# Last stage of a transformer block: order of two first loads, PSUM tags of one plain product, and two banks for the last accumulator

## The chip, the core and the metric

The kernel runs on one core of one Trainium2 chip. The metric is device time in microseconds (us) of one execution; the median of eight runs of the kernel before is 760.04 us (758.58 to 761.81). Engines are named as in the profile: PE is TensorE, DVE is VectorE, ACT is ScalarE, POOL is GpSimd, SP is SyncE. SP and ACT also issue DMA transfers, each from its own queue, in the order of their programs.

## The reference

Input x is 2048 tokens by 1024 features in bf16. The block is

```
h  = x + linear_attention(layernorm(x)) @ wo
h2 = h + (relu(g) * u) @ W_down       where g = layernorm(h) @ W_gate, u = layernorm(h) @ W_up
```

W_gate and W_up are 1024 by 3584, W_down is 3584 by 1024. The change touches the last product alone, called the Down stage here: with hh = relu(g) * u (2048 by 3584), it computes out = h + hh @ W_down.

## The kernel before

Each large product is done by the Winograd form of Strassen's scheme: both matrices are cut into 2 by 2 blocks, sums and differences of blocks are formed, and seven block products take the place of eight. In the Down stage this is done on two levels.

**Outer level.** hh is cut into halves of 1024 tokens and 1792 inner features, W_down into halves of 1792 rows and 512 columns. The seven outer products run in the order `OUTER = (1, 2, 6, 5, 3, 7, 4)` (line 808); n is the place in this order, from 0 to 6. The block sums of the left side were written to DRAM by the stage before ("spilled", `x_dram`, lines 661 and 668) and come back by `load_x` (line 833); W_down itself, or sums of its blocks from `t_dram`, come by `load_w` (line 820). One `load_x` or `load_w` is 896 KB: 128 partitions of seven rows of 512 bf16 numbers. A spilled tile is ready in DRAM when its last row has been written; the last row of all is written by line 668 at the very end of the stage before.

**Inner level.** Outer products 2, 6, 5, 3 and 4 (`INNER`) are again done by the seven-product scheme (`inner`, line 1081): each inner product `mm` (line 1098) is 512 tokens by 896 by 256, that is 4 token tiles of 128 times 7 slices of the inner features, 28 matmuls of 128x256. Outer products 1 (n = 0) and 7 (n = 5) are done plainly, in four pieces p of two token tiles, each 2 times 14 matmuls of 128x512 (`plain_mm`, line 930).

**Accumulators.** PSUM holds four accumulators of two banks each ([128, 1024] fp32): two of tag A, one of tag X, one of tag Y. In an inner product m1, m6, m7 and m4 are added up in one A, with a copy taken by DVE between them (`snap`, line 1109, which also adds the running sum `base`); m2 has X or Y by the parity of n (`tag`, line 1084), and so has m5, in the same accumulator as soon as m2 has been read; m3 is added onto m5. A product that adds onto an accumulator must wait for the copy that reads it; a product that takes an accumulator anew must wait for the last reader of its former content. In the plain product at n = 5 the four pieces use A, A, Y and X (line 1244).

**Order.** PE, DVE and ACT run in the order in which the program is written (`manual_schedule`, line 745), SP too in the Down stage (line 964). The sums of an outer product's operands (t1, s1, s2, t2, s4, s3, t3, t4, lines 1018 to 1045) stand in `queue`, and `pop()` puts the next one into DVE's order between the copies. So at n = 1 three such sums of the next product, t1, s1 and s2, stand in DVE's order after the addition "00" that follows m2 and ahead of the copy "s2" (`snap` of u2), which frees A for m7.

**The last outer product** (n = 6, `tail`) has no successor to overlap with. It ends with m7, a copy, m4 in the other A accumulator ("m4f"), additions for the four output quadrants (`sink`, which calls `put`, line 1064), and m3 in two halves of two token tiles ("m3a", "m3b"), each followed by its addition ("01a", "01b"). `put` adds accumulator and copy into a bf16 tile (line 1069), adds h where that was not done earlier (line 1071), and stores with a DMA from ACT's queue (line 1073). m5, m3a and m3b all live in one accumulator of tag X.

Of the kernel before, what the change touches and what calls it, by code (L numbers as in the profile page):

```python
# [31 lines left out]
def block_kernel(ctx: ExitStack, tc: tile.TileContext, x, wqkv, wo, wg, wu, wd, out, H: int):  # L32
# [178 lines left out]
    with ExitStack() as actx:  # L211
# [11 lines left out]
        def load_x(t):  # L223
            x_sb = bwork.tile([P, D], BF16, tag=("x_res", "oT")[atiles.index(t) % 2], bufs=XB, name="x_sb")
            nc.sync.dma_start(out=x_sb[:], in_=xf[t * P:(t + 1) * P, :])
            x_tiles[t] = x_sb

        def load_w(dst, j, col):
            nc.sync.dma_start(out=dst[:, :, j * NW:(j + 1) * NW], in_=wqkv_v[:, :, col + j * NW:col + (j + 1) * NW])
# [744 lines left out]
    def new_op(n):  # L974
        return {"n": n, "k": OUTER[n], "s": {}, "t": {}}
# [18 lines left out]
    def pop(n=1):  # L994
        for _ in range(n):
            if queue:
                queue.pop(0)[2]()
# [63 lines left out]
            nc.scalar.dma_start(out=v[:], in_=h_dram[i][s][:, :, j * DW:(j + 1) * DW])  # L1061
            hres[k, s] = v

    def put(k, s, ts, cs, ps, m, with_h=True):

        i, j = outs[k]
        o = dpool.tile([P, NT * HW], BF16, tag="o", bufs=4, name="o")
        ov = o[:, 0:(ts.stop - ts.start) * (cs.stop - cs.start)].rearrange("p (t d) -> p t d", t=ts.stop - ts.start)
        add(out=ov, in0=ps, in1=m, op=ALU.add)  # L1069
        if with_h:  # L1070
            add(out=ov, in0=ov, in1=hres[k, s][:, ts, cs], op=ALU.add)  # L1071
        t0 = (i * HS + s * SW) // P
        nc.scalar.dma_start(out=out_v[:, t0 + ts.start:t0 + ts.stop, j * DW + cs.start:j * DW + cs.stop], in_=ov)

    def cols(j):
        return slice(j * HW, (j + 1) * HW)
# [4 lines left out]
    def inner(op):  # L1081

        k, st, base = op["k"], {}, base_of[op["k"]]
        tag = "XY"[op["n"] % 2]

        def left(m):
            return {1: x_tile(op["n"], 0, 0), 2: x_tile(op["n"], 0, 1), 3: op["s"].get("s4"), 4: x_tile(op["n"], 1, 1),
                    5: op["s"].get("s1"), 6: op["s"].get("s2"), 7: op["s"].get("s3")}[m]

        def right(m):  # L1090
            w = [w_tile(op["n"], x) for x in range(2)]
            return {1: w[0][:, :, cols(0)], 2: w[1][:, :, cols(0)], 3: w[1][:, :, cols(1)], 4: op["t"].get("t4"),
                    5: op["t"].get("t1"), 6: op["t"].get("t2"), 7: op["t"].get("t3")}[m]

        def view(nm):
            return st[nm][:].rearrange("p (t d) -> p t d", t=NT)

        def mm(m, nm, t=None, ts=range(NT)):
            need(op, *{3: ("s4",), 4: ("t4",), 5: ("s1", "t1"), 6: ("s2", "t2"), 7: ("s3", "t3")}.get(m, ()))
            if t:  # L1100
                st[nm] = acc(t)
            pv = view(nm)
            for tt in ts:
                for f in range(FQ):
                    nc.tensor.matmul(pv[:, tt, :], lhsT=left(m)[:, f, tt * P:(tt + 1) * P], rhs=right(m)[:, f, :],  # L1105
                                     start=(t is not None and f == 0 and tt % 2 == 0),
                                     stop=(f == FQ - 1), skip_group_check=True)

        def snap(nm, s, j):
            st[nm] = dpool.tile([P, NT, HW], FP32, tag="snap", bufs=4, name="snap")  # L1110
            add(out=st[nm][:], in0=view("A"), in1=base[s][:, :, cols(j)], op=ALU.add)  # L1111

        def add_h(m, s, j):
            add(out=st[m][:], in0=st[m][:], in1=hres[k, s][:, :, cols(j)], op=ALU.add)

        def sink(s, j, nm, m, ts=ALL, with_h=True):
            m = base[s][:, ts, cols(j)] if m is None else st[m][:, ts]
            if k in u_of:
                add(out=u_of[k][s][:, ts, cols(j)], in0=view(nm)[:, ts], in1=m, op=ALU.add)
            else:  # L1120
                put(k, s, ts, cols(j), view(nm)[:, ts], m, with_h)

        return {
            "m1": lambda: mm(1, "A", "A"), "s1": lambda: snap("m1", 0, 0), "m2": lambda: mm(2, "D", tag),
            "00": lambda: sink(0, 0, "D", "m1"), "m6": lambda: mm(6, "A"), "s2": lambda: snap("u2", 0, 1),
            "m5": lambda: mm(5, "E", tag), "m7": lambda: mm(7, "A"), "s3": lambda: snap("u3", 1, 1),
            "11": lambda: sink(1, 1, "E", "u3"), "m4": lambda: mm(4, "A"), "10": lambda: sink(1, 0, "A", None),
            "m3": lambda: mm(3, "E"), "01": lambda: sink(0, 1, "E", "u2"),
            "m4f": lambda: mm(4, "F", "A"), "10f": lambda: sink(1, 0, "F", "u3f"), "snap": snap,
            "01a": lambda: sink(0, 1, "E", "u2", slice(0, 2), False),  # L1130
            "01b": lambda: sink(0, 1, "E", "u2", slice(2, 4), False), "h01": lambda: add_h("u2", 0, 1),
            "m3a": lambda: mm(3, "E", None, (0, 1)), "m3b": lambda: mm(3, "E", None, (2, 3)),
        }

    ops = [new_op(n) for n in range(len(OUTER))]
    load_x(1, 1, 1, slice(0, FQ - 1))
    load_x(1, 1, 1, slice(FQ - 1, FQ))
    load_w(1, 0)
    load_w(1, 1)
    load_x(1, 0, 1)  # L1140
    queue_sums(ops[1])

# [24 lines left out]
    for n in range(1, len(OUTER)):  # L1167
        op = ops[n]
        nxt = ops[n + 1] if n + 1 < len(OUTER) else None
        tail = nxt is None  # L1170

        def early_loads():
            if nxt and n > 1:
                load_w(n + 1, 0)
                load_x(n + 1, 1, 0)

        def late_x():
            if nxt and n > 1:
                load_x(n + 1, 1, 1)

        def late_w():
            if nxt and n > 1:
                load_w(n + 1, 1)
                if nxt["k"] in INNER:
                    queue_sums(nxt)

        def ahead():
            if n + 2 < len(OUTER):
                need(op, "s4")
                load_x(n + 2, 0, 0)  # L1190
                load_x(n + 2, 0, 1)

        early_loads()
        if op["k"] in INNER:
            cur = inner(op)
            cur["m1"]()
            if prv:
                prv["11"]()
                pop()
            cur["s1"]()  # L1200
            cur["m2"]()
            if prv:
                prv["m4"]()
            late_x()
            cur["00"]()
            pop()
            if prv:
                prv["10"]()
                prv["m3"]()
            late_w()  # L1210
            pop()
            cur["m6"]()
            if prv:
                prv["01"]()
            pop()
            if nxt:
                load_h(nxt["k"], 0)
                if op["k"] not in outs:
                    load_h(nxt["k"], 1)
            cur["m5"]()  # L1220
            cur["s2"]()
            if tail:
                cur["h01"]()
            pop(2)
            cur["m7"]()
            ahead()
            pop(2)
            if tail:
                cur["snap"]("u3", 1, 1)
                cur["m4f"]()  # L1230
                cur["11"]()
                cur["snap"]("u3f", 1, 0)
                cur["m3a"]()
                cur["10f"]()
                cur["01a"]()
                cur["m3b"]()
                cur["01b"]()
            else:
                cur["s3"]()
            prv = cur  # L1240
        else:
            pss = []
            for p in range(4):
                ps = acc(("A", "A", "XY"[n % 2], "XY"[(n + 1) % 2])[p])
                plain_mm(ps, n, p, 0)
                plain_mm(ps, n, p, 1)
                if p == 0 and prv:
                    prv["11"]()
                    prv["m4"]()
                    late_x()  # L1250
                    prv["10"]()
                    prv["m3"]()
                    late_w()
                    prv["01"]()
                    load_h(op["k"], 1)
                s, t0 = divmod(2 * p, NT)
                ts = slice(t0, t0 + 2)
                v = ps[:].rearrange("p (t d) -> p t d", t=2)
                put(op["k"], s, ts, full, v, u5[s][:, ts, :])
                add(out=u2[s][:, ts, :], in0=v, in1=u2[s][:, ts, :], op=ALU.add)  # L1260
                pop(2)
            if nxt:
                load_h(nxt["k"], 0)
                load_h(nxt["k"], 1)
            prv = None
# [46 lines left out]
```

## Time and profile before

| What | us |
|---|---|
| median of 8 runs | 760.04 (758.58 to 761.81) |
| the profiled execution's own time | 761.81 |
| its span, first to last instruction | 760.0 |
| time around the span | 1.8 |
| PE busy in the span | 731.6 (96%) |
| DVE busy in the span | 567.4 (75%) |
| Down stage in the span | from about 585 to 760 |

Times inside the profile are counted from the start of the span. A line of the timeline has the start, the duration, the engine, the line of the kernel, the operation, the tiles written and read, the shape, the number of merged instructions, and in brackets the idle time of the engine before it with what ended it. Matmuls overlap, so a run of them ends for the next engine a little before its printed end. The granted clock (PEclk) is the share of TensorE's full clock that the chip allowed; it averages 0.987 over the span.

### The profile page before, as it was taken

The numbers are of one execution on the slowest core, as the hardware profiler recorded it, in microseconds if no ns is written. First come the engines' busy times: TensorE is split into PE (matmuls) and PEld (weight loads), VectorE is DVE, ScalarE is ACT, GpSimd is POOL, SyncE is SP. The second block draws the span as 40 slices with busy tenths as digits, with TensorE's granted clock in tenths as the row PEclk, the third lists the DMA queues.
The fourth block names the chain that finished last, engine by engine and source line by source line (L and its number), as shares of the span: only waits on it lengthen the run. The fifth ranks groups of instructions, "written<-read, shape, count | busy, mean of one in ns | idle before, by whom it ended". The sixth has DMA issues, their size and how long they took to land. (4 is left out here: it accounts for less than half of the span.)

```text
span 760.0 us, 10598 instructions
## 1 busy us (share of the span) xinstructions
PE 731.6 (96%) x3967; PEld 385.0 (51%) x4020; DVE 567.4 (75%) x1023; ACT 324.4 (43%) x596; POOL 5.8 (1%) x44
## 2 busy tenths in 40 slices
PE   8999999999889989999999999999999999999986
PEld 3444555444344434444444444444444468887565
DVE  6997645786886756778777787797786398994784
ACT  4785664877777544434344443444443110000000
POOL 0000000000000000000000000000000000000000
PEclk9999999999999999999999999999999999999998
DMA  9755003099767526165628277594482697978631
GB/s 318 168 124 153 1 0 111 1 212 209 175 148 185 126 62 201 42 197 136 199 92 248 99 219 237 179 290 167 161 268 84 235 361 266 328 279 317 209 94 46
DMA packets 146563, 132.03 MB, mean 174 GB/s; under 512 B 50896, under 2 KB 128080, under 8 KB 146512
## 3 DMA queue, kind: packets, MB, share of 16 engines
q1 hardware_dynamic: 134848, 122.97, 53.2%
q10 hardware_dynamic: 11664, 8.39, 3.6%
q8 instruction: 31, 0.51, 0.3%
q14 instruction: 20, 0.16, 0.1%
HBM read 79.95 MB, written 39.85 MB: 158 GB/s over the span
## 5 line engine op out<-in xcount | busy, mean ns | idle before, releaser
L783 ACT ACTIVATE gu<-gu 128x512 bf16<-128x512 bf16 x72 | 45.4, 630 | 131.9 <-DVE gu L782 127.4
L778 ACT COPY snap<-accA 128x1024 f32<-128x1024 f32 x72 | 72.4, 1008 | 37.0 <-PE accA L773 37.0
L536 PE MATMUL attn<-wo_mem,oT 128*128 128x512 bf16 x247 | 59.0, 387 | 4.1 <-DVE o_sb L516 3.2
L773 PEld LDWEIGHTS <-tg 128*128 128x128 f16 x384 | 37.5, 98 | 45.3
L773 PEld LDWEIGHTS <-tu 128*128 128x128 f16 x384 | 37.6, 98 | 45.3
L153 ACT COPY u<-Aq 128x512 f32<-128x512 f32 x56 | 32.2, 581 | 44.6 <-PE Aq L297 19.3
L782 DVE TENSOR_TENSOR gu<-accY,snap 128x1024 bf16<-128x1024 f32 x36 | 43.8, 1218 | 9.8 <-ACT snap L778 9.6
L773 PE MATMUL accA<-hn,tu 128*128 128x512 f16 (+1 forms) x192 | 49.3, 379 | 0.0
L773 PE MATMUL accA<-hn,tg 128*128 128x512 f16 (+1 forms) x192 | 49.3, 379 | 0.0
L782 DVE TENSOR_TENSOR gu<-accX,snap 128x1024 bf16<-128x1024 f32 x36 | 43.9, 1218 | 7.2 <-PE accX L773 4.7
L1105 PEld LDWEIGHTS <-x 128*128 128x128 f16 (+1 forms) x448 | 44.5, 100 | 9.1 <-issue 2.9
L773 PEld LDWEIGHTS <-wg 128*128 128x128 bf16 x288 | 28.2, 98 | 34.9 <-issue 1.1
L773 PEld LDWEIGHTS <-wu 128*128 128x128 bf16 x288 | 28.2, 98 | 34.0
L536 PEld LDWEIGHTS <-oT 128*128 128x128 bf16 x256 | 25.4, 99 | 36.2 <-issue 8.8
L1105 PEld LDWEIGHTS <-xs 128*128 128x128 f16 x308 | 30.2, 98 | 3.6
L786 DVE TENSOR_TENSOR hq<-gu 128x512 bf16<-128x512 bf16 x48 | 20.3, 422 | 14.3 <-ACT gu L783 14.2
L297 PEld LDWEIGHTS <-xT 128*128 128x128 bf16 (+1 forms) x192 | 18.6, 98 | 23.5 <-issue 2.1
L516 DVE TENSOR_TENSOR o_sb<-nd,rd 128x384 bf16<-128x384 f32 (+1 forms) x48 | 22.8, 506 | 8.6 <-ACT rd L515 7.5
L538 DVE SCALAR_TENSOR_TENSOR x_res<-attn,x_res 128x512 bf16<-128x512 f32 x32 | 22.0, 688 | 8.8 <-PE attn L536 8.7
L1111 DVE TENSOR_TENSOR snap<-accA,u 128x1024 f32<-128x1024 f32 x16 | 19.5, 1218 | 11.5 <-PE accA L1105 11.5
L1105 PEld LDWEIGHTS <-xd 128*128 128x128 f16 (+1 forms) x224 | 23.1, 103 | 8.8 <-issue 5.0
L934 PEld LDWEIGHTS <-x 128*128 128x128 bf16 (+1 forms) x168 | 16.4, 98 | 19.8
(225 smaller groups left out, 1417.3 us busy)
## 6 DMA issues: line engine op xcount, KB each, us to landing
x<-x_dram SPq DMA_DIRECT2D x17, 896.0 KB, 8.7
x_dram<-hq SPq DMA_DIRECT2D x28, 512.0 KB, 3.0
wg<-in_B_W_gate_dram SPq DMA_DIRECT2D x14, 512.0 KB, 5.1
wu<-in_B_W_up_dram SPq DMA_DIRECT2D x14, 512.0 KB, 7.2
wraw<-in_B_W_down_dram SPq DMA_DIRECT2D x14, 512.0 KB, 5.1
x_dram<-hq SPq DMA_DIRECT2D x28, 256.0 KB, 2.5
t_dram<-wt SPq DMA_DIRECT2D x28, 256.0 KB, 2.2
xd<-x_dram SPq DMA_DIRECT2D x6, 896.0 KB, 5.9
```

The lines of the kernel that those rows point to most:

```text
L153: nc.scalar.copy(out=snaps[nm, v], in_=A[v][:])
L297: nc.tensor.matmul(ps[:], lhsT=left[m - 1][:, kc, r + v * P:r + (v + 1) * P], rhs=right[m - 1][:, kc, :], start=(start and kc == 0), stop= ...
L516: nc.vector.tensor_tensor(out=ov[:, c0:c0 + n], in0=ndv[:, :, 0:P].rearrange("p k (h e) -> p k h e", h=HPC), in1=rd[:, 0:n, :].unsqueeze(3 ...
L536: nc.tensor.matmul(ps[:], lhsT=st["oT"][:, c, :], rhs=wo_sb[:, c, j * NW:(j + 1) * NW], start=(c == 0), stop=(c == KC - 1))
L538: nc.vector.scalar_tensor_tensor(out=h_sb[:, j * NW:(j + 1) * NW], in0=ps[:], scalar=1.0, in1=h_sb[:, j * NW:(j + 1) * NW], op0=ALU.mult, ...
L773: nc.tensor.matmul(ps[:, v, :], lhsT=w[v][n - 1][:, kc, :], rhs=left[n - 1][:, kc, :], start=(t is not None and kc == 0), stop=(kc == KH - ...
L778: nc.scalar.copy(out=st[nm][:], in_=halves(st["A"]))
L782: add(out=g[:], in0=halves(st[nm]), in1=st[base][:], op=ALU.add)
L783: nc.scalar.activation(out=g[:, 0, :], in_=g[:, 0, :], func=ACT.Relu)
L786: add(out=out[q], in0=st[q][:, 0, :], in1=st[q][:, 1, :], op=ALU.mult)
L1105: nc.tensor.matmul(pv[:, tt, :], lhsT=left(m)[:, f, tt * P:(tt + 1) * P], rhs=right(m)[:, f, :], start=(t is not None and f == 0 and tt % ...
L1111: add(out=st[nm][:], in0=view("A"), in1=base[s][:, :, cols(j)], op=ALU.add)
```

## The change

Four places of the Down stage are edited.

1. Before the loop, the first loads at n = 1 are put in another order: first the weights w(1,0), then the first six rows of the spilled tile x(1,1,1), then the weights w(1,1), and then the last row of x(1,1,1).
2. In the plain product at n = 5 the third piece takes tag X and the fourth Y, in place of Y and X.
3. In the last product, m5 and m3 are written into two accumulators, two token tiles in the first bank of X and two in the first bank of Y (`tail_mm`); the additions that follow (`tail_sink`) go by these halves, and the store of the first half is issued from SP's queue in place of ACT's. m3 is not interrupted by other work any more: it runs as one piece after the addition "11".
4. In the last product, h for the second token half is added ahead of time to the running sum `u2[1]`, in one addition of 128x2048 after "h01"; the separate additions of h after "11" and "10" go.

```
-    def put(k, s, ts, cs, ps, m, with_h=True):
+    def put(k, s, ts, cs, ps, m, with_h=True, eng=nc.scalar):
...
-        nc.scalar.dma_start(out=out_v[...], in_=ov)
+        eng.dma_start(out=out_v[...], in_=ov)
...
+        def tail_mm(m, start):
+            need(op, *{3: ("s4",), 5: ("s1", "t1")}[m])
+            for h in range(2):
+                if start:
+                    st["E", h] = acc("XY"[(op["n"] + h) % 2])
+                for tt in range(2):
+                    for f in range(FQ):
+                        t = 2 * h + tt
+                        nc.tensor.matmul(st["E", h][:, tt * HW:(tt + 1) * HW],
+                                         lhsT=left(m)[:, f, t * P:(t + 1) * P], rhs=right(m)[:, f, :],
+                                         start=(start and f == 0 and tt == 0), stop=(f == FQ - 1),
+                                         skip_group_check=True)
+
+        def tail_sink(s, j, h, m):
+            ts = slice(2 * h, 2 * h + 2)
+            put(k, s, ts, cols(j), st["E", h][:, 0:2 * HW].rearrange("p (t d) -> p t d", t=2), st[m][:, ts],
+                False, (nc.sync, nc.scalar)[h])
...
+            "m5f": lambda: tail_mm(5, True), "m3f": lambda: tail_mm(3, False),
+            "11f": lambda: [tail_sink(1, 1, h, "u3") for h in range(2)],
+            "01f": lambda: [tail_sink(0, 1, h, "u2") for h in range(2)],
...
-            "m4f": lambda: mm(4, "F", "A"), "10f": lambda: sink(1, 0, "F", "u3f"), "snap": snap,
+            "m4f": lambda: mm(4, "F", "A"), "10f": lambda: sink(1, 0, "F", "u3f", ALL, False), "snap": snap,
...
+    load_w(1, 0)
     load_x(1, 1, 1, slice(0, FQ - 1))
+    load_w(1, 1)
     load_x(1, 1, 1, slice(FQ - 1, FQ))
-    load_w(1, 0)
-    load_w(1, 1)
     load_x(1, 0, 1)
...
-            cur["m5"]()
+            cur["m5f" if tail else "m5"]()
             cur["s2"]()
             if tail:
                 cur["h01"]()
+                add(out=u2[1][:], in0=u2[1][:], in1=hres[op["k"], 1][:], op=ALU.add)
...
                 cur["snap"]("u3", 1, 1)
                 cur["m4f"]()
-                cur["11"]()
+                cur["11f"]()
+                cur["m3f"]()
                 cur["snap"]("u3f", 1, 0)
-                cur["m3a"]()
                 cur["10f"]()
-                cur["01a"]()
-                cur["m3b"]()
-                cur["01b"]()
+                cur["01f"]()
...
-                ps = acc(("A", "A", "XY"[n % 2], "XY"[(n + 1) % 2])[p])
+                ps = acc(("A", "A", "XY"[(n + 1) % 2], "XY"[n % 2])[p])
```

More of the change, by code (lines that the diff above doesn't have):

```diff
@@ L1072, in put @@
         t0 = (i * HS + s * SW) // P
-        nc.scalar.dma_start(out=out_v[:, t0 + ts.start:t0 + ts.stop, j * DW + cs.start:j * DW + cs.stop], in_=ov)
+        eng.dma_start(out=out_v[:, t0 + ts.start:t0 + ts.stop, j * DW + cs.start:j * DW + cs.stop], in_=ov)
     def cols(j):
@@ L1128, in inner @@
             "m3": lambda: mm(3, "E"), "01": lambda: sink(0, 1, "E", "u2"),
-            "m4f": lambda: mm(4, "F", "A"), "10f": lambda: sink(1, 0, "F", "u3f"), "snap": snap,
-            "01a": lambda: sink(0, 1, "E", "u2", slice(0, 2), False),
-            "01b": lambda: sink(0, 1, "E", "u2", slice(2, 4), False), "h01": lambda: add_h("u2", 0, 1),
-            "m3a": lambda: mm(3, "E", None, (0, 1)), "m3b": lambda: mm(3, "E", None, (2, 3)),
+            "m4f": lambda: mm(4, "F", "A"), "10f": lambda: sink(1, 0, "F", "u3f", ALL, False), "snap": snap,
+            "h01": lambda: add_h("u2", 0, 1),
         }
     ops = [new_op(n) for n in range(len(OUTER))]
+    load_w(1, 0)
     load_x(1, 1, 1, slice(0, FQ - 1))
+    load_w(1, 1)
     load_x(1, 1, 1, slice(FQ - 1, FQ))
-    load_w(1, 0)
-    load_w(1, 1)
     load_x(1, 0, 1)
```

## The prediction

> **What bounds the kernel now.** The page says PE: 96% busy, and at least nine tenths in nearly every slice of the Down stage. So only PE's waits there, and the work behind its last matmul, can be won. I read PE's waits from 610 to 760 us next. There are three, and the change has one part for each:
>
> ```profile
> PE accX L1105 <- issue: 2.6, 1, 2.6
> PE accX L1105 <- DVE o L1069: 2.5, 1, 2.5
> PE accA L1105 <- DVE snap L1111: 2.1, 1, 2.1
> ```
>
> PE's timeline shows what each wait costs beyond itself:
>
> ```profile
> 627.45 4.88 PE L1105 MATMUL accA<-w,xd 128*128 128x256 f16 x28 [2.11 <-DVE snap L1111]
> 632.17 3.22 PE L1105 MATMUL accA<-wd,x 128*128 128x256 f16 x28
> ...
> 732.48 4.88 PE L1105 MATMUL accX<-wd,x 128*128 128x256 f16 x28 [2.61 <-issue]
> ...
> 753.60 2.55 PE L1105 MATMUL accX<-wd,xd 128*128 128x256 f16 x14 [2.49 <-DVE o L1069]
> ```
>
> 28 matmuls normally print 3.22 us and the next product starts 3.06 us later. After each wait they print 4.88 (1.66 more), and the 14 after the third 2.55 in place of 1.69 (0.86 more). The reason is in the windows; the columns are the stretch and its length, busy time by engine, and then the granted clock:
>
> ```profile
> 218.37:221.78 3.41, 1.69 (x13) 0.97 (x12) 3.41 (x12) 1.44 (x7) 0.00 (x0) 1.00 0.62 92
> 221.78:225.20 3.42, 3.15 (x14) 1.46 (x15) 2.19 (x7) 2.97 (x7) 0.00 (x0) 1.00 0.71 217
> ...
> 624.56:627.97 3.41, 1.30 (x13) 1.01 (x11) 3.41 (x3) 0.00 (x0) 0.00 (x0) 1.00 0.43 102
> 627.97:631.38 3.41, 3.41 (x18) 2.45 (x17) 3.41 (x3) 0.00 (x0) 0.00 (x0) 0.50 0.90 353
> ```
>
> Time is cut into fixed stretches of 3.41 us. A stretch with PE idle for 2.11 us is followed by one at half clock; one with 1.72 us is not, one with 1.90 (201.30 to 204.72) is. I take 1.8. The edges stand fixed in time, so it is chance whether a wait of 2.1 to 2.6 us lies mostly in one stretch. The full price of a half-clock stretch is 1.7 us.
>
> Here the Trainium skill differs ("TensorE: Matmul & The Clock Gate", section "HAM oscillation — how this bites in real kernels"). It says that idle gaps up to about 3.4 us are harmless. By it the 1.66 and 0.86 would not exist, and the sum would hold the third wait and the small costs below alone, 761.81 - 2.49 + 0.5 = 759.8, an estimate; the rows above decide against it.
>
> **Part 1, the loads.** DVE's timeline at n = 1:
>
> ```profile
> 605.64 1.09 DVE L1022 TENSOR_TENSOR ws<-w 128x1792 f16<-128x1792 bf16 x1 [10.03 <-DMA w<-in_B_W_down_dram]
> 606.65 2.02 DVE L1035 TENSOR_TENSOR xd<-xd,x 128x3584 f16<-128x3584 bf16 x1
> ...
> 617.52 1.22 DVE L1111 TENSOR_TENSOR snap<-accA,u 128x1024 f32<-128x1024 f32 x1
> 619.26 1.22 DVE L1069 TENSOR_TENSOR o<-accY,snap 128x1024 bf16<-128x1024 f32 x1 [0.52 <-PE accY L1105]
> ...
> 626.18 1.22 DVE L1111 TENSOR_TENSOR snap<-accA,u 128x1024 f32<-128x1024 f32 x1
> ```
>
> t1 waits for w(1,0), issued at 598.32 and 7.3 us on its way. With w first, issued in the first load's place at 596.11, t1 goes some 5 us earlier. But the backlog does not reach the first wait: DVE idles 0.52 at 619.26 for PE's m2, and from there to the copy's end (619.26 to 627.40, 8.14 us: "00", h, then t1, s1, s2 of the next product, then the copy) it runs without a break, while PE has only m6 and m5, 6.1 us. Nothing in these 8.14 us moves, and DVE's order is the same in the changed kernel. So the first wait stays at 2.11, and part 1 gains nothing.
>
> It may cost. s1 (606.65) needs all of x(1,1,1), whose last row now queues behind both weights. SP held that row until 597.94 (the spill's landing), so it, w(1,1) and x(1,0,1) change places but not in number. In the profile the four loads (2.75 MB) were all in at 598.80 plus 9.4 = 608.2 (the pair of w has a median of 8.4, the first 7.3). If the last row lands as late as that, s1 starts at 608.2 in place of 606.65; if the queue gains from starting on w at once, 606.3. s1 has 0.5 us to spare (the idle time at 619.26). The bounds are 0 and 1.1 us of longer first wait; I take 0.2, since the transfer rate in 597 to 599 was 250 to 270 GB/s against 315 to 345 later, which an earlier w would partly fill. The loads behind keep their place and are released by PE at 601 and 613.
>
> **Part 2, the swap.** Before the last product:
>
> ```profile
> 724.30 1.22 DVE L1260 TENSOR_TENSOR u<-accY,u 128x1024 f32<-128x1024 f32 x1
> ...
> 731.16 1.22 DVE L1260 TENSOR_TENSOR u<-accX,u 128x1024 f32<-128x1024 f32 x1
> 732.29 1.08 DVE L1029 TENSOR_TENSOR wd<-wd 128x1792 f16<-128x1792 f16 x1
> 733.29 1.08 DVE L1032 TENSOR_TENSOR ws<-wd,ws 128x1792 f16<-128x1792 f16 x1
> 734.30 1.22 DVE L1111 TENSOR_TENSOR snap<-accA,u 128x1024 f32<-128x1024 f32 x1
> ```
>
> m2 waited for X until 732.38. With the tags swapped X is free at 725.52, and m2 follows m1 at 729.71 and ends at 732.76. But m6 is added onto the A that the copy at 734.30 reads, and that copy ends at 735.52, behind DVE work that is packed from 708.72 on and does not change. So PE waits again, before m6 in place of m2: from 732.93 (printed end) to 735.57, 2.64 us where it was 2.61. At full clock m2 would have ended at 735.54 in the old order too; the swap alone is worth nothing there. In the profile m6 started at 737.19, so m6 comes 1.62 us earlier, and whether the half clock falls on m6 instead is open: of the new wait 1.79 us lies in the stretch 733.78 to 737.19, between 1.72 and 1.90.
>
> **Parts 3 and 4, the end.** From m6's start to the last addition's start the profile has 737.19 to 756.19, 19.00 us. New: m6, m5, m7, m4, m3 without a break, 5 times 3.06 = 15.3, and 0.2 from PE's end to DVE (as m6, next start 740.25, to its copy at 740.46): 15.5. Gain 3.5: the 2.49 wait, the 0.86 of clock, and little else.
>
> What could break this run, with m6 at 735.57: m5 needs X read by "00" (735.56 + 1.23 = 736.8, against 738.6) and Y read by the fourth piece (732.4); m7 needs the copy of u2 (738.84 to 740.06, against 741.7). Then DVE has h01 (1.23, line 1114's row) and the new addition of 128x2048; 128x1024 of the same types took 1.23, so 1.2 to 2.5, I take 2.3: done by 743.6, hidden under m7, whose copy starts at 744.96; beyond 3.6 us it would push that copy one for one. It needs h of the second half, issued at 732.26 and landed by 737.6. "11" is two additions of 0.68 (the row at 752.87), done at 746.9 and 747.6 against 747.8 and 749.3 when m3's halves want their banks. The copy u3f, "10" and the first "01" end at 750.8; the last "01" waits for PE until 751.1. The two h additions (0.69 each) go from DVE's tail; they were not on the path beyond the wait already counted.
>
> Behind the last addition the profile has 3.81 us (756.19 to 760.0): addition, issue, landing 1.8, end. Three stores now start within 1.7 us; the two that overlapped before took 2.3 and 2.2 against 1.8 alone, so I add 0.3 (bounds 0 and 0.5). The SP queue is empty by then (its last load was at 708.71), so its two stores hold nobody up. The Trainium skill ("DMA: Bandwidth & Descriptors", section "Issuing engines are not separate DMA queues") says that issuing from several engines saves only issue time, so by it the SP store is worth at most the 0.38 us of an issue and only if ACT is busy; no run here shows it yet.
>
> **Sum.** Against the profiled execution (761.81, span 760.0): -1.62 - 3.5 + 0.3 + 0.2 = -4.6, so 757.2 if m6 keeps the full clock, 758.9 if not. The profile had all three waits followed by half clock and lies 1.77 over the median. So I take the half clocks out: before 761.81 - 1.66 - 1.66 - 0.86 = 757.6, after 757.2 - 1.66 = 755.5; and put them back by chance. With 1.8 as the limit, a wait of g us escapes when an edge splits it into two parts that are both under 1.8. That is so for 3.6 - g of the 3.41 us over which the edge can lie: 44% for 2.11, 29% for 2.61, 33% for 2.49. Before: 757.6 + 0.56 x 1.66 + 0.71 x 1.66 + 0.67 x 0.7 = 760.2, against the median 760.04, which supports the reading. After: 755.5 + 0.93 + 0.72 x 1.66 = 757.6; since a split half clock partly falls into the wait itself, I take 0.4 off: **757.2 us**, 2.8 (0.4%) under the median.
>
> **Rivals.**
> - *The last row comes late* (part 1 costs 1 to 3 us): first wait 3 to 5 us, always at half clock. For it: w(1,0) took 7.3 us, a later w of the same size 4.9. Against: the same four loads, earlier started. 758.5 to 760.
> - *Part 1 removes the first wait*, since DVE's 10.03 us of idle time are its root: 757.2 - 2.11 - 0.93 = 754.2. Against: the 0.52 us at 619.26.
> - *Part 3 doesn't do what it says*: m3 still waits, now for "11", because the new addition is far slower than its row: 2.5 back, 759.7. Against: 3.6 us of room.
> - *Slower than before*: the last row's landing passes 607.1 by more than 4.5 us (after 611.6); each further us delays s1, the copy and m7 by one. At 614 that is 757.2 + 6.9 - 0.2 = 763.9. Against: by then even x(1,0,1), queued behind, had landed (599.45 + 11.2 = 610.7).
>
> **Chances.** Forecast 0.74, late row 0.11, first wait gone 0.06, third wait stays 0.05, slower 0.04. The forecast's own bounds are 755.2 (no half clock, no extra store time) and 759.3 (755.5, two half clocks, 0.4 more for the row); the range reaches to 759.6 for the late row and leaves out 754.2 and the slower case. A measurement tells 0.2% (1.5 us) from no change: faster means under 758.5. Faster 0.84 (nearly all of the forecast, the gone wait, some of the late row), same 0.12, slower 0.04.
>
> **What would show it.** First wait on the copy at line 1111 unchanged at 2.1 or slightly more, with t1 some 5 us earlier. No wait of m2; a new one of 2.6 before m6, released by line 1111. No wait inside m3. The last addition 15.5 us after m6's start at full clock. The forecast is wrong if s1 starts after 607.1, if m6 starts before the copy could have run, or if DVE's last copies run behind PE.

## The result and the profile after

The changed kernel takes 754.98 us (median of 24 runs, 753.3 to 759.22) against 759.44 us (66 runs, 756.0 to 763.38) of the kernel before on the same chips. The ratio is 0.9944, with a 95% interval of 0.9932 to 0.9956: 3.3 to 5.2 us faster. The forecast was 757.2 us and a range from 755.2; the measured median lies 0.2 us below that range. The direction was right and the gain was half as large again as forecast (0.56% against 0.4%).

The profiled execution took 756.25 us with a span of 754.5. PE's waits from 590 us on, in the changed kernel (columns: total, times, longest):

```profile
PE accA L1105 <- DVE snap L1111: 4.8, 2, 2.6
```

Two waits are left of three, and both are for a DVE copy. PE's timeline of the changed kernel:

```profile
625.28 4.88 PE L1105 MATMUL accA<-w,xd 128*128 128x256 f16 x28 [2.11 <-DVE snap L1111]
...
727.53 3.22 PE L1105 MATMUL accX<-wd,x 128*128 128x256 f16 x28
733.39 4.88 PE L1105 MATMUL accA<-ws,xs 128*128 128x256 f16 x28 [2.64 <-DVE snap L1111]
738.11 1.69 PE L1131 MATMUL accX<-ws,xs 128*128 128x256 f16 x14
...
747.28 1.69 PE L1131 MATMUL accX<-wd,xd 128*128 128x256 f16 x14
748.81 1.69 PE L1131 MATMUL accY<-wd,xd 128*128 128x256 f16 x14
```

The first wait, before m7 of n = 1, is 2.11 us as before. m2 of the last product follows m1 without a wait, and the wait stands before m6 instead, 2.64 us long. m3 runs in one piece. In this execution both waits are followed by a stretch at half clock (the 4.88 in place of 3.22). DVE's end of the changed kernel:

```profile
740.71 2.28 DVE L1243 TENSOR_TENSOR u<-u,h 128x2048 f32<-128x2048 f32 x1
744.43 1.23 DVE L1111 TENSOR_TENSOR snap<-accA,u 128x1024 f32<-128x1024 f32 x1 [1.43 <-PE accA L1105]
...
750.54 0.69 DVE L1069 TENSOR_TENSOR o<-accY,snap 128x512 bf16<-128x512 f32 x1 [0.52 <-PE accY L1131]
```

The new addition of h takes 2.28 us, and DVE still idles for 1.43 us behind it: it is hidden.

Against the profile before, 5.5 us of span are gone, in two parts. One is not the change's. The Down stage's first inner product starts at 612.95 before and at 610.78 after, though nothing ahead of it was edited but the order of four loads, on which PE does not wait there. The windows from 200 to 210 and 270 to 280 us show the cause, in the kernel before

```profile
200.00:210.00 10.00, 7.16 (x31) 2.98 (x31) 8.37 (x26) 5.02 (x20) 0.00 (x0) 0.83 0.44 104
270.00:280.00 10.00, 8.36 (x31) 3.46 (x31) 4.37 (x11) 4.68 (x10) 0.00 (x0) 0.83 0.25 67
```

and in the changed kernel

```profile
200.00:210.00 10.00, 6.43 (x36) 2.93 (x35) 9.55 (x29) 6.32 (x21) 0.00 (x0) 1.00 0.75 165
270.00:280.00 10.00, 9.20 (x42) 4.18 (x43) 4.82 (x13) 4.87 (x12) 0.00 (x0) 1.00 0.19 42
```

The column before the last two is the granted clock: 0.83 over 10 us is one stretch of 3.41 us at half clock. The execution before had two such stretches ahead of the Down stage and the one after had none: most of the 2.17 us, which come and go with the execution. (Two later profiles without half clock ahead of the stage, of variants of the changed kernel, start that product at 611.32 and 611.47 us, so up to 0.7 us of the 2.17 can be other spread.) The rest, 760.0 - 612.95 = 147.05 against 754.5 - 610.78 = 143.72, is 3.33 us, and that is the change: the third wait (2.49) and its half clock (0.86) make 3.35.

### The profile page after: what moved, and what is told of

Its sections match the earlier page's. It is cut to its first block, busy times and chain, and to the rows that moved or that the text cites. A ratio compares the mean times of both kernels' runs of the same rounds, so it can differ in the third digit from the quotient of the medians.

```text
span 754.5 us, 10599 instructions
## 1 busy us (share of the span) xinstructions
PE 726.2 (96%) x3967; PEld 383.4 (51%) x4020; DVE 568.1 (75%) x1023; ACT 324.7 (43%) x596; POOL 5.8 (1%) x44
## 5 line engine op out<-in xcount | busy, mean ns | idle before, releaser
L536 PE MATMUL attn<-wo_mem,oT 128*128 128x512 bf16 x247 | 57.3, 379 | 4.1 <-DVE o_sb L516 3.2
L1105 PEld LDWEIGHTS <-xs 128*128 128x128 f16 x280 | 28.2, 101 | 6.8 <-issue 2.8
L773 PE MATMUL accA<-hn,wg 128*128 128x512 bf16 x73 | 23.3, 379 | 2.0 <-DVE gu L702 0.8
```

What stands on the lines that cost most here:

```text
L536: nc.tensor.matmul(ps[:], lhsT=st["oT"][:, c, :], rhs=wo_sb[:, c, j * NW:(j + 1) * NW], start=(c == 0), stop=(c == KC - 1))
L773: nc.tensor.matmul(ps[:, v, :], lhsT=w[v][n - 1][:, kc, :], rhs=left[n - 1][:, kc, :], start=(t is not None and kc == 0), stop=(kc == KH - ...
```

## Experiments

Five kernels isolate the parts and the clock, three more take the waits that are left, and one asks about the store queue. Times are compared as ratios to the kernel before, run on the same chip.

### The loads alone

```
-    load_x(1, 1, 1, slice(0, FQ - 1))
-    load_x(1, 1, 1, slice(FQ - 1, FQ))
     load_w(1, 0)
+    load_x(1, 1, 1, slice(0, FQ - 1))
     load_w(1, 1)
+    load_x(1, 1, 1, slice(FQ - 1, FQ))
```

> The kernel before with the new order of the four first loads alone. Theory A (the first wait is set by what DVE does after m2, so the loads do nothing): time unchanged within 0.5 us (ratio 0.9995 to 1.0005), the wait before m7 of n = 1 still 2.1 us, t1 some 5 to 6 us earlier, s1 within 1 us of its old place, three PE waits as before. Theory B (the part of the gain that was not forecast, about 1.4 us, came from the loads): 1 to 2 us faster, and the first wait shorter than 2.1 us.

Measured: 759.04 us, ratio 0.9991 (0.9976 to 1.0006). DVE's timeline of this kernel:

```profile
600.40 1.09 DVE L1022 TENSOR_TENSOR ws<-w 128x1792 f16<-128x1792 bf16 x1 [5.93 <-DMA w<-in_B_W_down_dram]
605.37 2.02 DVE L1035 TENSOR_TENSOR xd<-xd,x 128x3584 f16<-128x3584 bf16 x1 [3.87 <-DMA x<-x_dram]
```

t1 starts 11.40 us before the first inner product (at 611.80 here), where it started 7.31 before it: 4.1 us earlier, not the 5 to 6 expected. s1 then waits 3.87 us for the spilled rows and starts 6.43 us before that product, against 6.30: no earlier worth the name. The wait before m7 is 2.12 us. The loads do nothing to the end, as theory A said.

### The swap alone

```
-                ps = acc(("A", "A", "XY"[n % 2], "XY"[(n + 1) % 2])[p])
+                ps = acc(("A", "A", "XY"[(n + 1) % 2], "XY"[n % 2])[p])
```

> The kernel before with the swapped tags of the plain product alone. Theory A (the wait only moves from m2 to m6): no wait of m2, a wait of 2.6 us before m6 released by the copy at line 1111, the third wait of 2.5 us still inside m3; time 0 to 0.5 us faster. Rival (the swap removes the wait): 2.5 to 4 us faster, and m6 follows m2 without a wait.

Measured: 758.61 us, ratio 0.9996 (0.9979 to 1.0014). PE's timeline of the swap alone:

```profile
728.57 3.22 PE L1105 MATMUL accX<-wd,x 128*128 128x256 f16 x28
734.44 3.22 PE L1105 MATMUL accA<-ws,xs 128*128 128x256 f16 x28 [2.64 <-DVE snap L1111]
...
750.84 1.69 PE L1105 MATMUL accX<-wd,xd 128*128 128x256 f16 x14 [2.49 <-DVE o L1069]
```

and of the loads alone, which have the old tags:

```profile
731.34 3.22 PE L1105 MATMUL accX<-wd,x 128*128 128x256 f16 x28 [2.61 <-issue]
...
750.83 1.69 PE L1105 MATMUL accX<-wd,xd 128*128 128x256 f16 x14 [2.49 <-DVE o L1069]
```

These two profiles happen to be an exact pair: each has one half-clock stretch ahead of the Down stage and one after the first wait, none at the second or third, and both spans are 756.4 us. With 2.61 us of waiting before m2 or 2.64 before m6, the second half of m3 starts at 750.83 and 750.84. The swap moves the wait and gains nothing.

### The new end alone

Parts 3 and 4 of the change (two banks, h added early, SP store) with the old loads and tags.

> The kernel before with the new end of the last product alone (two banks, h added early, SP store). Theory A: this is nearly the whole gain, 3.4 to 4.3 us faster (2.5 of wait, the rest half clock that no longer follows), no wait inside m3, the waits before m7 of n = 1 and before m2 of the last product as before. Rival (the three parts share the gain): at most 2.5 us faster, with the rest in the other two.

Measured: 756.21 us, ratio 0.9957 (0.994 to 0.9975), 3.3 us faster by the ratio. That falls just under theory A's 3.4 and above the rival's 2.5, and the interval (1.9 to 4.6 us) reaches into both. PE's waits of this kernel from 590 us on are the first two alone, with nothing inside m3:

```profile
PE accX L1105 <- issue: 2.6, 1, 2.6
PE accA L1105 <- DVE snap L1111: 2.1, 1, 2.1
```

Together with the two runs above, whose intervals both contain no change, this part carries nearly all of the gain. Parts 3 and 4 were not run apart. The two additions of h that part 4 takes away (0.69 us each) stood in DVE's packed order ahead of the addition that the third wait was for, so how much of the 2.49 us either part alone would win is open.

### Matmuls in the waits

In the changed kernel PE gets matmuls with nothing to do in its two waits, into an accumulator that is free (for the last product, m4's accumulator is taken early, and m4 overwrites it):

```
+        def warm(t, nn, m):
+            ps = acc(t)
+            for q in range(nn):
+                nc.tensor.matmul(ps[:, 0:128], lhsT=left(m)[:, 0, 0:P], rhs=right(m)[:, 0, 0:128],
+                                 start=True, stop=True, skip_group_check=True)
+            return ps
...
+            if tail:
+                cur["warm2"]()
             cur["m6"]()
...
+            if n == 1:
+                cur["warm1"]()
             cur["m7"]()
```

> The changed kernel with matmuls of 128x128 into an unused accumulator in the two waits that are left (18 before m7 of n = 1, 23 before m6 of the last product; their sums are thrown away). They take work in no one's place: the copies that PE waits for end when they did. Theory A (a fixed stretch in which PE idles for more than 1.8 us is followed by 3.41 us at half clock): no half clock follows either place, m7 and m6 start when they did, counted from the waits' beginnings, and the time falls 1 to 2 us below the changed kernel, that is 5 to 6.5 us under the kernel before. Rival (the slower matmuls after a wait come from the wait itself, such as cold weights or a late semaphore): the 28 matmuls behind the places still print 4.9 us and the time stays at the changed kernel's, or grows.

Measured: 753.58 us (752.81 to 754.83), ratio 0.992 (0.9903 to 0.9938). PE's timeline of this kernel:

```profile
626.20 3.22 PE L1105 MATMUL accA<-w,xd 128*128 128x256 f16 x28 [1.11 <-DVE snap L1111]
...
729.85 1.45 PE L1144 MATMUL accA<-ws,xs 128*128 128x128 f16 x23
732.65 3.22 PE L1105 MATMUL accA<-ws,xs 128*128 128x256 f16 x28 [1.36 <-DVE snap L1111]
```

m6 is not earlier: it starts 5.86 us after m2, as in the changed kernel (733.39 - 727.53). But its 28 matmuls print 3.22, and so do m7's. In this profile a wait of which 1.4 us or less is idle is not followed by half clock. By the medians the kernel is 1.4 us under the changed one, within theory A's 1 to 2. Its six runs spread over 2.0 us; the changed kernel's 24 spread over 5.9 (of more runs, so the two are not quite comparable). The slow matmuls behind a wait are the clock's, not the wait's.

The same was done to the kernel before, in its three waits (28, 35 and 33 matmuls):

> The kernel before with matmuls of 128x128 into an unused accumulator in all three waits (28, 35 and 33 of them, their sums thrown away), so that PE never idles long there. Theory A: the waits' ends stay, no half clock follows, and the time is that of the kernel before less its half clocks: 3 to 4 us under it, 755.5 to 756.5. Set against the changed kernel filled in the same way (5.8 us under the kernel before), the difference, 2 to 3 us, is what the change is worth without the clock. Rival (the third wait alone made the whole gain of 4.4 us): the difference is over 4 us.

Measured: 756.66 us, ratio 0.997 (0.995 to 0.999). Its third wait's length is as before, less what the added matmuls occupy. For m2's wait this profile names what the kernel before has only as "issue", the addition that reads the plain product's fourth piece (L1282 here, L1260 there):

```profile
732.04 3.23 PE L1105 MATMUL accX<-wd,x 128*128 128x256 f16 x28 [0.62 <-DVE u L1282]
...
748.94 2.02 PE L1126 MATMUL accA<-wd,xd 128*128 128x128 f16 x33
751.58 1.69 PE L1105 MATMUL accX<-wd,xd 128*128 128x256 f16 x14 [0.62 <-DVE o L1069]
```

The median lies just above the expected 755.5 to 756.5. The two filled kernels differ by 3.1 us by the medians and by 3.8 by the ratios, between theory A's 2 to 3 and the rival's 4; most runs still had half clocks elsewhere, in earlier stages in the profiles. Some runs of both had no half clock anywhere (granted clock 1.0 over the span). These compare the two kernels without the clock:

| Kernel | runs at full clock | time, us | span, us (mean) |
|---|---|---|---|
| before, waits filled | 2 of 12 | 755.46, 755.47 | 753.7 |
| changed, waits filled | 3 of 6 | 752.81, 753.13, 753.33 | 751.27 |

Without the clock the change is worth 2.4 us, the third wait (2.49). By the medians, half clocks in the filled places cost the kernel before 759.64 - 756.66 = 3.0 us and the changed one 754.98 - 753.58 = 1.4; these are from different sets of runs, and with the intervals of the ratios each is uncertain by about 1.5 us. 2.4 and 1.6 make 4.0 of the 4.3 us that the ratio gives. The granted clock of single runs, on record for 47 of the kernel before and 25 of the changed one, points the same way with more runs: at a clock of 0.995 the mean times are 758.35 us (12 runs) and 755.35 (10), 3.0 apart, and at 0.998 they are 756.71 (4) and 754.09 (10), 2.6 apart (at 0.993, with only two runs of the changed kernel, 2.0). The rest of the 4.3 us, some 1.3 to 1.7, is clock: its mean is 0.9929 before and 0.9958 after.

### The two waits that are left

The first wait is DVE's order at n = 1. This kernel takes the copy of u2 ahead of s1 and s2 of the next product:

```
             late_w()
-            pop()
+            if n > 1:
+                pop()
             cur["m6"]()
...
-            pop()
+            if n > 1:
+                pop()
...
-            pop(2)
+            pop(2 if n > 1 else 4)
             cur["m7"]()
```

> The changed kernel with another order on DVE at n = 1: the copy of u2 comes after t1 of the next product, ahead of its s1 and s2, which follow later. Theory A (the first wait is DVE's order after m2): the wait of 2.1 us before m7 goes, and the half clock after it, and nothing else waits longer than 0.5 us: 2 to 3.5 us under the changed kernel, 751.5 to 753. Rival (DVE is behind by the same amount and the wait comes back at the next copy, before m4 inside n = 2): at most 1 us under it, with a wait of about 2 us there.

Measured: 753.86 us, ratio 0.9923 (0.9892 to 0.9953). The wait before m7 is gone, and part of it is back one product later, as the timeline of PE shows:

```profile
623.95 3.22 PE L1105 MATMUL accA<-w,xd 128*128 128x256 f16 x28
...
646.60 3.22 PE L1105 MATMUL accA<-wd,x 128*128 128x256 f16 x28 [0.85 <-DVE snap L1111]
```

Here 2.11 us became 0.85, at m7 of n = 2 and not at m4 as the rival had it; with six runs, 1.1 us under the changed kernel by the medians is between the two expectations. DVE has no slack there: in this profile it has no listed idle time from 618.04 us to the copy at 645.33 that m7 waits for, so a copy moved forward pushes the sums behind it.

The wait before m6 of the last product is DVE's order, too. t3 and t4 are left in the queue over the plain product's fourth piece:

```
-                pop(2)
+                if p < 3:
+                    pop(2)
             if nxt:
```

> The changed kernel with the sums t3 and t4 of the last product left in the queue over the fourth piece of the plain product, so that the copy of m1 comes 2.0 us earlier on DVE. Theory A (the swap moved the wait to m6, and DVE's order sets it): the wait before m6 falls from 2.64 to about 0.6 us, too short for a half clock: 2 to 3.5 us under the changed kernel, 751.5 to 753. Rival (the sums are missed later: m7 or m4 wait for them): a new wait of 1 us or more there, and at most 1 us gained.

Measured: 753.65 us, ratio 0.9915 (0.9889 to 0.9942). PE's timeline:

```profile
732.09 3.22 PE L1105 MATMUL accA<-ws,xs 128*128 128x256 f16 x28 [0.64 <-DVE snap L1111]
738.56 3.22 PE L1105 MATMUL accA<-wd,x 128*128 128x256 f16 x28 [0.20 <-DVE snap L1111]
```

The wait is 0.64 as expected, with 0.20 new before m7. By the medians it is 1.3 us under the changed kernel, below theory A's 2 to 3.5; the ratio gives 2.2. Both orders in one kernel:

> The changed kernel with both new orders on DVE, of n = 1 and of the last product. Theory A: the gains add up, since the places are 100 us apart: no wait of PE over 0.7 us in the Down stage, no half clock there, 4 to 6.5 us under the changed kernel, 748.5 to 751, and a narrow spread of runs. Rival (a later wait takes up part of it): 752 or more.

Measured: 751.31 us (750.94 to 753.56), ratio 0.9897 (0.987 to 0.9923): the fastest kernel of this study, 1.0% under the kernel before and 3.7 us under the changed one. PE's waits in the Down stage (total, times, longest):

```profile
PE accA L1105 <- DVE snap L1111: 1.7, 3, 0.8
```

The 0.85, the 0.64 and 0.16 are still there, so the median lies a little above the expected 748.5 to 751, and the gain below the expected 4. No half clock falls in the Down stage of this profile; its one half-clock stretch is at 204 us, in an earlier stage.

### The store queue

Both stores of the split additions from ACT: `(nc.sync, nc.scalar)[h]` goes from `tail_sink`.

> The changed kernel with both stores of the split additions issued from ACT, as before the change. Theory A (the stores take the same time from either queue, and ACT is free by then): the last store is issued when the last addition ends, lands 1.8 to 2.0 us later, and the stretch from the last addition's start to the end of the span stays at 3.8 to 4.0 us. Rival (ACT's queue is late with the store before it): the last store is issued 0.4 us or more after the addition ends and the stretch grows by as much.

Measured, one execution (755.13 us, span 753.3). DVE's timeline:

```profile
748.22 0.68 DVE L1069 TENSOR_TENSOR o<-accX,snap 128x512 bf16<-128x512 f32 x1
749.42 0.69 DVE L1069 TENSOR_TENSOR o<-accY,snap 128x512 bf16<-128x512 f32 x1 [0.52 <-PE accY L1131]
```

From the last addition's start to the end of the span it is 753.3 - 749.42 = 3.88 us, against 754.5 - 750.54 = 3.96 with the SP store. With one execution of each, the SP store shows no gain: the two additions end at 748.90 and 750.11 us, and ACT issues their stores at 748.93 and 750.14. That agrees with the Trainium skill ("DMA: Bandwidth & Descriptors", section "Issuing engines are not separate DMA queues"), by which a second queue saves issue time alone.

## Why the prediction was right and wrong, point by point

**First wait, part 1.** Right: 2.11 us in both profiles. t1 came 4 us earlier, not 5, and the last row cost 0, not 0.2: s1 starts 6.30 us before the first inner product in both traces. The rival of the late row did not happen, nor did the slower case.

**The swap.** Right to the hundredth: no wait of m2, 2.64 us before m6, nothing gained at full clock. The new wait was followed by half clock in the profile after (its stretch has 2.28 us of idle time), not in that of the swap alone.

**The end.** Right. 15.5 us were forecast from m6 to the last addition at full clock. The changed kernel has 750.54 - 733.39 = 17.15 with one half clock (1.66), 15.49 without it. The new addition was taken at 2.3 and is 2.28. Only the stores were mis-sized: 0.3 was added, and 3.96 - 3.81 = 0.15 came.

**The base without half clocks: here the level failed.** The prediction took three half clocks out of the profiled 761.81 and got 757.6 before and 755.5 after. The same execution had two more, at 204.72 and 272.98 us; the prediction even named the window ahead of the first to find its limit, and left both in the base. Their price was some 1.5 to 2.2 us, by the start of the first inner product above. With all five out, 761.81 - 4.18 - 2.17 = 755.5, or up to 0.7 more, and less the third wait 753.0. The filled kernels' executions at full clock were 755.46 and 755.47, and 752.81 to 753.33: the base was 2.1 us too high. The range's lower end, 755.2, stood on it; 2.2 us lower it would have been 753.0, under the measured 754.98.

**Half clocks by chance: here the gain failed.** The prediction put back 2.6 us for the three waits before and, with the 0.4 that it took off, 1.7 for the two after. No run shows the 0.4, and it was taken off on one side only. The medians say 3.0 and 1.4, so 1.6 of gain in place of 0.9, and the single runs at the same clock leave 1.3 to 1.7. The limit of 1.8 us was too low as well: an idle time of 2.05 us in a stretch had no half clock behind it in the profile of the new end alone. That makes each chance smaller, so the chances alone don't explain the measured 3.0. Nor is every wait a matter of chance as the prediction had it: the first wait of 2.11 us, unfilled, was followed by half clock in all seven profiles that have it, which a chance of 0.56 would give one time in 60. The stretch's edge fell 0.02 to 0.91 us behind the wait's end in each; why is not shown. That raises both levels and leaves the gain alone. The agreement that was taken for support, 760.2 by the sum against 760.04, was luck, two errors that cancel: a base 2.1 too high, and too little put back for chance, in the earlier stages and here. In the gain, the base cancels; the missing 1.5 us are some 0.4 to 0.8 of clock, 0.35 of costs that did not come (0.2 for the row, 0.15 for the stores), and the rest within the uncertainty.

**Rivals.** That the loads remove the first wait is refuted by the run of the loads alone; that the third wait stays is refuted by every profile with the new end.

## What to carry to other kernels

Before a wait is removed, ask what else the waiting engine needs next: swapping two buffers moved PE's wait from one product to the following one, since the copy that the following one needs stood later in the same packed DVE order, while reordering that order shortened the wait. A PE wait of 2.1 to 2.6 us cost up to 1.7 us more in clock here, so one execution's profile is a base only after every half-clock stretch in its whole span has been taken out, not just those near the change. When the wait itself can't go, matmuls with nothing to do in it bought 1.4 us here by the medians.

## What the runs showed of the hardware

The half-clock rule, over all the profiles of this case: time is cut into stretches of 3.41 us (the half-clock stretches of the kernel before begin at 204.72, 272.98, 627.97, 733.78 and 754.26 us, whole multiples of 3.413 apart). Of the stretches at full clock that end before PE's last matmul does, one with 2.11 us or more of idle PE time was always followed by one at half clock (16 of 16). Below 1.90 us it never was; from 1.90 to 2.05 both happened. Two windows of the new end alone show a case just under it:

```profile
729.71:733.13 3.42, 1.37 (x13) 1.26 (x14) 3.39 (x5) 0.00 (x0) 0.00 (x0) 1.00 0.41 120
733.13:736.54 3.41, 3.41 (x33) 3.03 (x32) 3.15 (x4) 0.00 (x0) 0.00 (x0) 1.00 0.76 263
```

PE is busy for 1.37 of 3.42 us there, and the clock stays at 1.00. So the Trainium skill's "no PE-idle gaps" over about 3.4 us ("TensorE: Matmul & The Clock Gate", section "HAM oscillation — how this bites in real kernels") is too mild here: a gap of 2.11 us was enough whenever it lay in one stretch. That shorter gaps are harmless is how the prediction read that rule. Also not expected: 23 matmuls of 128x128 with the same operand took 1.45 us, 63 ns each, and leaving 1.36 us of the wait idle was enough to keep the full clock.
